# Spreading the short products of a Fourier stage between the long products of a matrix stage

## The chip, the cores and the metric

The kernel runs on one core of a Trainium2 chip. A core has five engines, each with a queue of its own: TensorE (PE in the profile; its weight loads are listed apart as PEld), VectorE (DVE), ScalarE (ACT), GpSimd (POOL) and SyncE (SP), which here only issues transfers. The metric is the device time of one execution in microseconds (us), from the first to the last instruction of the core. Every time below is either such a device time, or is read from a trace of one profiled execution. A product takes two operands: the one that stays in the array ("weights", loaded by a PEld instruction) and the one that streams through it, column by column.

## What is computed

Eight sequences of 3008 rows by 256 columns are transformed by a two-dimensional discrete Fourier transform, of which only the real part is kept. Each row of the result then goes through a two-layer network with a squared ReLU between.

```python
# x: (8, 3008, 256); w_in: (256, 2048); w_out: (2048, 256); all float32
X = np.fft.fft(np.fft.fft(x, axis=1), axis=2).real
t = X.reshape(8 * 3008, 256)
r = np.maximum(t @ w_in, 0.0)
out = (r * r) @ w_out
```

The kernel merges the transform along the 256 columns into `w_in` (the tables `G1` and `G2`). What is left of the transform, the one along the 3008 rows, is folded by sums and differences until only products of small cosine and sine tables are left; their results are joined again by sums and differences into two arrays, `Pt` and `Qt`. These are the streamed operand of the network.

## The kernel before

The main loop runs over 8 sequences, 6 blocks of 251 columns (the last has 250) and 8 pairs of hidden tiles `j`, 384 steps in all. A step has a `front` (four products of 251 columns, whose results VectorE combines), a `combine` on ScalarE and GpSimd, and a `back` (seven products of 251 columns), which belongs to the front of two steps earlier.

```python
def front(b, k0, n, j, between):
    ...
    for h in range(2):
        ...
        ps = psh.tile([P, 2, CH], F32, name="ph", tag="h")      # two buffers
        nc.tensor.matmul(hP, G1[:, fs], pt[:, ks], start=True, stop=True)
        nc.tensor.matmul(hQ, G2[0:P - 1, fs], qt[0:P - 1, ks], start=True, stop=True)
        nc.vector.scalar_tensor_tensor(out=t, in0=et[:, ks], scalar=gE[:, fc:fc + 1], in1=hP, ...)
        tt(out=g[:, h, 0, 0:n], in0=t, in1=hQ, op=ALU.add)
        tt(out=g[:, h, 1, 0:n][:, ::-1], in0=t, in1=hQ, op=ALU.subtract)
        between()
    return g
```

While sequence `b` goes through the network, sequence `b + 1` is transformed. Its work is a list `side` of pairs (weight, function), and `between()`, which each half of a front calls, takes from it. The weights set the pace: all of them together are spread evenly over a fixed number of calls (53 for the first list, 78 for each later one).

```python
def between():
    nonlocal spent
    if i < NJ + LAG or i % NJ == LAG - 1:
        return
    spent -= pace / 4 if i < 2 * NJ else pace
    while side and spent <= 0:
        t, f = side.pop(0)
        f()
        spent += t
...
    if i % per == 0:
        side = ahead(b + 1) if b + 1 < B else []
        calls = 2 * (NJ - 1) * (len(BLOCKS) - (0 if i else 2)) - 6 + (0 if i else (NJ - LAG) // 2)
        spent, pace = 0.0, sum(t for t, _ in side) / calls
```

The list begins with the folds, which are VectorE work for nearly all of it. For a tile of rows:

```python
        ops = [(0.9, f_s), (0.9, f_d), (0.7, f_sc), (0.6, f_dc), (1.1, f_w)]
        ...
        return ops + [(0.8, f_turn), (1.3 if odd else 0.7, f_even), (0.2, f_sine)], (1.4 if odd else 1.2, f_odd)
```

After them come four groups (`kp` 0 and 1, for the cosine and the sine). In each, `even_n` issues four products one after the other: one of row class 0 and one of class 1 (94 or 95 columns each), and two of class 2, each again of 94 or 95 columns, through `once_more`. `odd_n` issues four products of 188 or 189 columns. The `join` functions are VectorE sums and differences; `copy_4` is a ScalarE copy.

```python
            EVEN = ((0, 0, n2), (1, n2, n2), (2, 2 * n2, n1))

            def even_n():
                st["ps"] = psd.tile([P, 512], F32, name="pd", tag="d")[0:n]      # psd: two buffers
                for c, at, nk in EVEN:
                    if b and c == 2:
                        st["half"] = once_more(st["ps"][:, at:], c, nk)
                    else:
                        product(st["ps"][:, at:at + nk], c)
                copy_4()
            ...
            ops = [(0.1, even_n), (0.4, join_4), (0.5, join_2), (0.1, odd_n), (0.8, join_1)]
            if b and kp:
                ops.insert(4, (0.5, lambda: join_odd("odd", n0)))
                ops.insert(2, (0.4, lambda: join_odd("half", n1)))
            return ops
```

Sequence 0 has no side list; it is transformed before the loop starts. In the list for sequence 1 a small transform of one column of all later sequences (`b is None`, operand `we`, seven columns of weights) comes between the folds and the four groups.

Of the kernel before, what the change touches and what calls it, by code (L numbers as in the profile page):

```python
# [8 lines left out]
F32 = mybir.dt.float32  # L9
# [4 lines left out]
P = 128  # L14
# [68 lines left out]
def kernel(  # L83
# [43 lines left out]
    psd = ctx.enter_context(tc.tile_pool(name="psd", bufs=2, space=PSUM))  # L127
# [221 lines left out]
    def columns(tab, t, part):  # L349

        nk, at = NC[0][TILES[t][0]], PLACE[t]
        nq = (nk + 1) // 2
        return tab[:, 0, at + part * nq:at + (nk if part else nq)]
# [120 lines left out]
    def dft_ops(b):  # L474
# [7 lines left out]
        def group(kp, which):  # L482
            both_in = b == 0 and which == 1
            n = NE if b is None else P - 1 if which == 1 and b else P
            tab = sinT if which == 1 else cosT
            n2, _, n1, n0 = NC[kp]
            st = {}

            def product(ps, c, lone_e=False, only=None):

                ts = [t for t in range(NT) if TILES[t][0] == c]
                for t in ts if only is None else ts[only:only + 1]:
                    rows = TILES[t][3]
                    if b is None:
                        w = we[0:rows, kp, t, 0:n]
                    elif lone_e:
                        w = lone[0:rows, 2 * t + kp]
                    else:
                        w = folded[b, t][0:rows, kp, PART[which]]
                        w = w if which else w[:, 0:n]  # L500
                    nc.tensor.matmul(ps[0:w.shape[-1]], w,  # L501
                                     (cosT if lone_e else tab)[0:rows, kp, PLACE[t]:PLACE[t] + NC[kp][c]],
                                     start=t == ts[0] and (lone_e or not both_in), stop=t == ts[-1] and not lone_e,
                                     skip_group_check=both_in)

            EVEN = ((0, 0, n2), (1, n2, n2), (2, 2 * n2, n1))

            def even_n():
                st["ps"] = psd.tile([P, 512], F32, name="pd", tag="d")[0:n]
                for c, at, nk in EVEN:  # L510
                    if b and c == 2:
                        st["half"] = once_more(st["ps"][:, at:], c, nk)
                    else:
                        product(st["ps"][:, at:at + nk], c)
                copy_4()

            def copy_4():
                a = st["a"] = hp.tile([P, 2 * P], F32, name="da", tag="da", bufs=2)[0:n]
                nc.scalar.copy(a[:, 0:n2], st["ps"][0:n, 0:n2])
# [43 lines left out]
                    st["odd"] = pool.tile([P, 512], F32, name="pd", tag=tag)[:, 0:n0]  # L563
                product(st["odd"], 3, lone_e, i)

            def once_more(ps, c, nk):

                nq = (nk + 2) // 2 if kp else (nk + 1) // 2
                pairs, rows = ((((TWO, TWO + 1),), HALF2), (((ODD0, ODD0 + 1), (ODD0 + 2, NT)), P))[c == 3]
                for part in range(2):  # L570
                    if kp:
                        tab, o = (cosT, sinT)[part], 0
                        to = ps[:, part * nq:part * nq + nq]
                    else:
                        tab, o = (cosT, sinT)[which], part
                        to = ps[:, part:nk:2]
                    for i, pair in enumerate(pairs):
                        nc.tensor.matmul(to, folded[b, pair[part != which]][0:rows, kp, PART[which]][:, 0:n],  # L578
                                         columns(tab, pairs[0][i] if c == 3 else TWO, o)[0:rows],
                                         start=i == 0, stop=i == len(pairs) - 1)  # L580
                if not kp:
                    return ps[:, 0:nk]
                a = hp.tile([P, NC[0][3] // 2 + 1], F32, name="oc", tag="oc", bufs=1)[0:n, 0:nq]
                nc.scalar.copy(a, ps[:, 0:nq])
                return a, ps[:, nq:2 * nq]

            def odd_n():
                ps = psd.tile([P, 512], F32, name="pd", tag="d")[0:n]
                st["odd"] = ps[:, 0:n0]
                if b is None:  # L590
                    return product(ps[:, 0:n0], 3)
                st["odd"] = once_more(ps, 3, n0)

            def join_odd(what, nk):

                a, ps = st[what]
                nq = a.shape[-1]
                st[what] = o = hp.tile([P, NC[1][3]], F32, name="do", tag="do", bufs=1)[0:n, 0:nk]
                tt(out=o[:, 0::2], in0=a[:, 0:nq - 1], in1=ps[:, 0:nq - 1], op=ALU.add)
                if which == 1:  # L600
                    tt(out=o[:, 1::2], in0=ps[:, 1:nq], in1=a[:, 1:nq], op=ALU.subtract)
                else:
                    tt(out=o[:, 1::2], in0=a[:, 1:nq], in1=ps[:, 1:nq], op=ALU.subtract)
# [13 lines left out]
            if b == 0:  # L617
                named = [("join_4", join_4), ("join_2", join_2), ("lo", join_lo), ("hi", join_hi),
                         ("join_1", join_1)]
                for i in range(3):  # L620
                    for nm, f in (("even", even_part), ("odd", odd_part)):
                        named += [(nm + ("", "_e")[e] + str(i), lambda i=i, e=e, f=f: f(i, e == 1)) for e in range(2)]
                return [((which, kp, nm), f) for nm, f in named]
            ops = [(0.1, even_n), (0.4, join_4), (0.5, join_2), (0.1, odd_n), (0.8, join_1)]
            if b and kp:
                ops.insert(4, (0.5, lambda: join_odd("odd", n0)))
                ops.insert(2, (0.4, lambda: join_odd("half", n1)))
            return ops

        ops = [] if b is None else [(0.0, start)]  # L630
        for which in (2,) if b is None else (0, 1):
            for kp in range(2):
                ops += group(kp, which)
# [307 lines left out]
    for i in range(len(steps) + LAG + 4):  # L941
        if i < len(steps):
            b, k0, n, j = steps[i]
# [21 lines left out]
        if i >= LAG and flight:  # L965
            at, g_, s_ = flight.pop(0)
# [73 lines left out]
```

## Time and profile before

| what | value |
|---|---|
| device time, median of 3 runs | 1939.01 us (1938.49 to 1940.76) |
| span of the profiled run | 1936.6 us |
| VectorE busy | 1424.4 us, 74% |
| GpSimd busy | 1185.6 us, 61% |
| ScalarE busy | 939.5 us, 49% |

A line of instruction groups reads: source line, engine, operation, result <- operands, shape, count, then busy time in us and mean ns of one instruction. In a timeline the first two columns are start and length in us, and instructions of one kind that follow each other are merged into one line (`x4`). A float32 product is two matmul instructions in this trace, each with its own weight load; the text calls them passes. The end of a matmul is modelled by the profiler, so consecutive ones overlap in it; how long a pass really takes is read from the distance of starts. In a table by stretches (`A:B`) each engine has its busy time and, in brackets, its number of instructions.

### The profile page before, as it was taken

The page shows a single profiled execution, that of the slowest core. Times are in us where ns is not written, and L with a number is a line of the kernel's source. Part 1 is how long each engine was busy: PE and PEld are TensorE (multiplying, and loading weights), DVE is VectorE, ACT ScalarE, POOL GpSimd, SP SyncE. Part 2 cuts the span into 40 slices and gives each one's busy share as a digit, 9 for nine tenths or more (in the row PEclk, how much of TensorE's full clock was granted, in tenths as well). Part 3 has the DMA queues.
Part 4 walks back from the last instruction along what each step waited for, and adds up shares of the span by engine and source line. Part 5 has one row for each costly group of instructions (what it writes and reads, how often), then busy time and mean ns, then how long its engine had stood idle before and what let it go on. Part 6 is the DMA issues. An engine that isn't in the chain of part 4 may idle for free.

```text
span 1936.6 us, 27913 instructions
## 1 busy us (share of the span) xinstructions
PE 1922.7 (99%) x9266; PEld 1708.9 (88%) x9266; DVE 1424.4 (74%) x3502; ACT 939.5 (49%) x1134; POOL 1185.6 (61%) x1708
## 2 busy tenths in 40 slices
PE   8999999999999999999999999999999999999999
PEld 7788888888988899888998889888898888988887
DVE  8998867777677776787667776777767787655554
ACT  2855554544445544445444454445544454444443
POOL 0047646676567665766667665667756776556655
PEclk9999999999999999999999999999999999999999
DMA  8341101111011101111011100111001100000000
GB/s 216 115 48 41 39 8 51 33 32 27 27 41 31 38 12 30 39 41 28 11 35 47 36 20 11 42 48 28 20 17 52 33 11 22 28 12 11 22 11 22
DMA packets 145783, 69.56 MB, mean 36 GB/s; under 512 B 129309, under 2 KB 136423, under 8 KB 145638
## 3 DMA queue, kind: packets, MB, share of 16 engines
q1 hardware_dynamic: 145186, 66.87, 13.3%
q8 instruction: 73, 1.20, 0.3%
q0 software_dynamic: 176, 0.65, 0.1%
q14 instruction: 72, 0.59, 0.1%
q10 hardware_dynamic: 276, 0.26, 0.0%
HBM read 43.03 MB, written 24.69 MB: 35 GB/s over the span
## 4 chain that ended last, share of the span: by engine, by line
PE 95%; DVE 3%; DMA 1%; issue 0%; SPq 0%; ACT 0%; DVEq 0%
PE ph L664 17%; PE ph L665 16%; PE mC L717 16%; PE mA L717 16%; PE mB L717 16%; PE mD L717 8%; PE pd L578 2%; PE pd L501 1%; DMA cosT<-in_cos_s_dram 0%; DVE m L274 0%; DVE he L667 0%; DMA cosd<-in_cos_d_dram 0%; DVE fd L272 0%; DVE g L670 0%; PE mA L704 0%
## 5 line engine op out<-in xcount | busy, mean ns | idle before, releaser
L679 ACT ACTIVATE g<-g 128x1004 f32<-128x1004 f32 (+1 forms) x384 | 399.4, 1040 | 783.6 <-DVE g L670 419.1
L667 DVE SCALAR_TENSOR_TENSOR he<-Et,gE,ph 128x251 f32<-128x251 f32 (+1 forms) x768 | 361.6, 471 | 385.4 <-PE ph L665 382.0
L687 POOL TENSOR_TENSOR s<-g 128x251 f32<-128x251 f32 (+1 forms) x376 | 249.0, 662 | 640.6 <-ACT g L680 507.2
L664 PE MATMUL ph<-Pt,G 128*128 128x251 f32 (+1 forms) x1536 | 451.9, 375 | 0.2 <-DVE g L670 0.2
L665 PE MATMUL ph<-Qt,G 127*128 127x251 f32 (+1 forms) x1536 | 451.3, 374 | 0.0
L680 ACT ACTIVATE g<-g 128x1004 f32<-128x1004 f32 (+1 forms) x384 | 399.3, 1040 | 12.1
L717 PE MATMUL mC<-s,wsum 128*128 128x251 f32 (+1 forms) x1504 | 381.4, 374 | 0.0
L717 PE MATMUL mA<-g,wout 128*128 128x251 f32 (+1 forms) x1504 | 379.9, 374 | 0.0
L669 DVE TENSOR_TENSOR g<-he,ph 128x251 f32<-128x251 f32 (+1 forms) x768 | 320.5, 417 | 54.5 <-DVE he L667 0.9
L665 PEld LDWEIGHTS ph<-Qt,G 127*128 127x128 f32 x1536 | 291.3, 190 | 35.7
L664 PEld LDWEIGHTS ph<-Pt,G 128*128 128x128 f32 x1536 | 286.7, 189 | 36.2 <-DVE dc L547 1.3
L717 PEld LDWEIGHTS mC<-s,wsum 128*128 128x128 f32 x1504 | 285.5, 190 | 34.5
L670 DVE TENSOR_TENSOR g<-he,ph 128x251 f32<-128x251 f32 (+1 forms) x768 | 314.1, 409 | 0.0
L717 PEld LDWEIGHTS mA<-g,wout 128*128 128x128 f32 x1504 | 282.6, 189 | 35.0 <-issue 0.3
L689 POOL TENSOR_TENSOR s<-g 128x251 f32<-128x251 f32 (+1 forms) x376 | 303.3, 807 | 0.0
L688 POOL TENSOR_TENSOR s<-s,g 128x251 f32<-128x251 f32 (+1 forms) x376 | 280.1, 745 | 29.5
L690 POOL TENSOR_TENSOR s<-g,s 128x251 f32<-128x251 f32 (+1 forms) x376 | 260.6, 693 | 0.0
L717 PE MATMUL mB<-g,wsum 128*128 128x251 f32 (+1 forms) x752 | 220.4, 374 | 0.0
L717 PE MATMUL mD<-s,wout 128*128 128x251 f32 (+1 forms) x752 | 220.3, 374 | 0.0
L717 PE MATMUL mB<-s,wout 128*128 128x251 f32 (+1 forms) x752 | 219.9, 374 | 0.0
L717 PEld LDWEIGHTS mB<-g,wsum 128*128 128x128 f32 x752 | 142.5, 190 | 17.5
L717 PEld LDWEIGHTS mD<-s,wout 128*128 128x128 f32 x752 | 141.9, 189 | 17.7
(139 smaller groups left out, 1353.9 us busy)
## 6 DMA issues: line engine op xcount, KB each, us to landing
out_dram<-os SPq DMA_DIRECT2D x376, 56.0 KB
xt<-in_x_dram SPq DMA_DIRECT2D x25, 384.0 KB
xt<-in_x_dram SPq DMA_DIRECT2D x63, 128.0 KB
Et<-e_dram SPq DMA_DIRECT2D x7, 752.5 KB
xt<-in_x_dram SPq DMA_DIRECT2D x9, 512.0 KB
out_dram<-os SPq DMA_DIRECT2D x288, 6.8 KB
raw<-in_moe_w_in_dram SPq DMA_DIRECT2D x16, 256.0 KB
raw<-in_moe_w_out_dram SPq DMA_DIRECT2D x16, 256.0 KB
```

Source lines behind the costliest of these rows:

```text
L664: nc.tensor.matmul(hP, G1[:, fs], pt[:, ks], start=True, stop=True)
L665: nc.tensor.matmul(hQ, G2[0:P - 1, fs], qt[0:P - 1, ks], start=True, stop=True)
L667: nc.vector.scalar_tensor_tensor(out=t, in0=et[:, ks], scalar=gE[:, fc:fc + 1], in1=hP, op0=ALU.mult, op1=ALU.add)
L669: tt(out=g[:, h, 0, 0:n], in0=t, in1=hQ, op=ALU.add)
L670: tt(out=g[:, h, 1, 0:n][:, ::-1], in0=t, in1=hQ, op=ALU.subtract)
L679: act(v, v, AF.Relu)
L680: act(v, v, AF.Square)
L687: gt(out=s1, in0=g21, in1=g22, op=ALU.add)
L688: gt(out=s2, in0=s1, in1=g11, op=ALU.subtract)
L689: gt(out=s3, in0=g11, in1=g21, op=ALU.subtract)
L690: gt(out=s4, in0=g12, in1=s2, op=ALU.subtract)
L717: nc.tensor.matmul(acc[nm][:, i, 0:n], w, v[:, 0:n], start=j == 0 and i == 0, stop=j == NJ - 1, skip_group_check=True)
```

## The change

The lists of sequences 1 to 7 no longer have `even_n`. In its place stand four entries, each with one product of 94 or 95 columns and a weight of 0.6, so that `between()` hands them out at different calls, with products of 251 columns between them, as far as the pace allows. `even_n` stays for the small transform of one column. The products, their operands and their order are unchanged; `copy_4` comes after the second product and not after the fourth. The aim is that the weight loads of the short products and of what follows them can lie beside longer products. Since 2.4 stands in each group where 0.1 stood, the sum of the weights grows too, and with it the pace at which the whole list is handed out.

```diff
             def even_n():
                 st["ps"] = psd.tile([P, 512], F32, name="pd", tag="d")[0:n]
                 for c, at, nk in EVEN:
-                    if b and c == 2:
-                        st["half"] = once_more(st["ps"][:, at:], c, nk)
-                    else:
-                        product(st["ps"][:, at:at + nk], c)
+                    product(st["ps"][:, at:at + nk], c)
                 copy_4()
+            def even_0():
+                st["ps"] = psd.tile([P, 512], F32, name="pd", tag="d")[0:n]
+                product(st["ps"][:, 0:n2], 0)
+
+            def even_1():
+                product(st["ps"][:, n2:2 * n2], 1)
+                copy_4()
+
+            def half(part):
+                c, at, nk = EVEN[2]
+                st["half"] = once_more(st["ps"][:, at:], c, nk, part)
 ...
-            def once_more(ps, c, nk):
+            def once_more(ps, c, nk, only=None):
 ...
-                for part in range(2):
+                for part in range(2) if only is None else (only,):
 ...
-                if not kp:
+                if not kp or only == 0:
                     return ps[:, 0:nk]
 ...
-            ops = [(0.1, even_n), (0.4, join_4), (0.5, join_2), (0.1, odd_n), (0.8, join_1)]
-            if b and kp:
-                ops.insert(4, (0.5, lambda: join_odd("odd", n0)))
-                ops.insert(2, (0.4, lambda: join_odd("half", n1)))
-            return ops
+            ops = [(0.4, join_4), (0.5, join_2), (0.1, odd_n), (0.8, join_1)]
+            if not b:
+                return [(0.1, even_n)] + ops
+            if kp:
+                ops.insert(3, (0.5, lambda: join_odd("odd", n0)))
+                ops.insert(1, (0.4, lambda: join_odd("half", n1)))
+            return [(0.6, even_0), (0.6, even_1), (0.6, lambda: half(0)), (0.6, lambda: half(1))] + ops
```

## The prediction

> **What bounds the kernel now.** I read the page's first lines, then the waits of the steady part, then the timeline of TensorE around one group of short products, and last the table by stretches for VectorE.
>
> ```profile
> PE 1922.7 (99%) x9266; PEld 1708.9 (88%) x9266; DVE 1424.4 (74%) x3502; ACT 939.5 (49%) x1134; POOL 1185.6 (61%) x1708
> PE 95%; DVE 3%; DMA 1%; issue 0%; SPq 0%; ACT 0%; DVEq 0%
> ```
>
> The second line is the chain of work that ended last: 95% of the span is TensorE waiting for itself. The waits of the stretch from 480 to 1900 us say the same from the other side. All twenty lines of that answer have ScalarE, VectorE or GpSimd as the one that waits; the longest ones are these, and no PE or PEld line is among them:
>
> ```profile
> POOL s L687 <- ACT g L680: 400.3, 229, 4.4
> ACT g L679 <- DVE g L670: 335.2, 142, 4.2
> DVE he L667 <- PE ph L665: 321.5, 246, 3.0
> ```
>
> So in sequences 2 to 7 TensorE never waits for another engine. There the time is the sum of what its passes take, and a change can help only by making passes shorter. How long they take stands in the timeline (PE, then PEld) around one `even_n`:
>
> ```profile
> 466.05 0.58 PE L664 MATMUL ph<-Pt,G 128*128 128x251 f32 x2
> 466.47 0.59 PE L665 MATMUL ph<-Qt,G 127*128 127x251 f32 x2
> 466.90 0.58 PE L501 MATMUL pd<-cosT,w 95*128 95x95 f32 x4
> 467.32 0.61 PE L578 MATMUL pd<-cosT,w 94*128 94x95 f32 x4
> 467.76 0.62 PE L664 MATMUL ph<-Pt,G 128*128 128x251 f32 x2
> 468.22 0.59 PE L665 MATMUL ph<-Qt,G 127*128 127x251 f32 x2
> 468.64 0.59 PE L717 MATMUL mA<-g,wout 128*128 128x251 f32 x2
> ```
>
> ```profile
> 466.26 0.40 PEld L665 LDWEIGHTS ph<-Qt,G 127*128 127x128 f32 x2
> 466.69 0.62 PEld L501 LDWEIGHTS pd<-cosT,w 95*128 95x128 f32 x4
> 467.23 0.53 PEld L578 LDWEIGHTS pd<-cosT,w 94*128 94x128 f32 x4
> 467.68 0.30 PEld L664 LDWEIGHTS ph<-Pt,G 128*128 128x128 f32 x2
> ```
>
> A product of 251 columns takes 466.47 - 466.05 = 0.42 us for two passes; over longer stretches a pass is 0.212 us, which is 0.847 ns a column. A product of 189 columns (`odd_n`, at 477.14 us: eight passes in 1.28 us) takes 0.160 us a pass, again 0.847 ns a column. A pass of 95 columns would then take 0.080 us. It takes more: within the row the starts are 0.111 us apart (by end times, the eight distances here are 83, 111, 113, 111, 112, 112, 110, 112 ns, and the long pass after the row comes 243 ns after the last short one in place of 212). Eight passes and the two long ones after them need 468.22 - 466.90 = 1.32 us; taking off 0.425 leaves 0.895 us for the eight. So the row costs 0.895 - 8 x 0.080 = 0.25 us more than its columns. This is what the change is after.
>
> The reader is to see where in the row this excess arises. The first short pass is at full speed (83 ns): its weights were loaded during the long pass before it. Each weight load starts when the pass before it starts, 466.69 beside the long pass at 466.68 and so on, and never earlier. The excess therefore lies behind each short pass, not in front of it: a pass of 0.080 us is too short a cover for the next load, which needs 0.111. Eight short passes, eight such excesses of 31 ns; the eighth is paid by the long product behind the row (243 for 212).
>
> **What the Trainium skill says.** The page TensorE: Matmul & The Clock Gate, section Step-by-step: what each phase is for, says that a weight load can be pulled ahead of running matmuls into a background buffer, so that the next weights load while the present product runs. The trace agrees, and shows one load ahead, no more. The same page, section LDWEIGHTS (loading the stationary operand), gives columns / 1.2 ns whatever the number of rows: 107 ns for 128 columns. The trace has 111 ns as the distance in a row of short passes, with 94 and with 95 rows alike, though it lists each load with about 190 ns. The page Perfetto Trace Analysis, section Identifying the Most-Contended Engine, warns that matmul busy time isn't a measure of the distance to the best possible, and I use distances of starts for that reason.
>
> **The change part by part.**
>
> 1. Short products alone. One product is two short passes. Put between long ones, the first runs at 83.5 ns, the second ends 111.3 ns later (it loads its weights behind the first), and the long pass after it ends 242 ns later (its weights load behind the second). Together 436.8, less 212.4 for the long pass: 224.4 ns a product, 898 for four. The row of four today: 83.5 + 7 x 111.3 + 242 - 212.4 = 892 ns. So nothing is hidden that wasn't hidden: the number of passes that follow a short pass is eight in both. If anything, each new row adds 2 ns at its entry. With the weights and calls given I worked the lists through: for sequences 2 to 7 twelve of the sixteen short products come alone and four in pairs, 14 rows in place of 4; for sequence 1 most come in pairs. About 66 more rows at 2 ns: +0.1 us.
>
> 2. The pace in sequences 2 to 7. The weights add to 49.1 before and 58.3 after (4 x 2.3 more); over 78 calls the pace goes from 0.63 to 0.75, so the folds are handed out 19% more densely, and end earlier. VectorE has room: these rows of the table by stretches are the folds of sequence 3 and the groups after them,
>
> ```profile
> core 0: us, PE busy (x) PEld busy (x) DVE busy (x) ACT busy (x) POOL busy (x), PEclk, DMA share, GB/s
> 515.00:700.00 185.00, 185.00 (x874) 164.70 (x873) 140.51 (x333) 90.24 (x100) 126.46 (x177) 1.00 0.13 36
> 700.00:748.00 48.00, 48.00 (x250) 43.69 (x250) 32.59 (x91) 22.05 (x32) 26.24 (x40) 1.00 0.05 12
> ```
>
> 76% busy in the folds. The front's three operations (0.47, 0.42 and 0.41 us, about 1.3 a call, 2.34 us of TensorE apart) are some 100 of the 140 us; the other 40 grow by a fifth to 48 in the same time, 80%. No wait, 0 us.
>
> 3. The pace in sequence 1's list. Its weights are 56.2 before and 65.4 after, over only 53 calls: 1.06 and 1.23. Here VectorE is close to its limit already:
>
> ```profile
> 142.00:182.00 40.00, 40.00 (x190) 35.58 (x189) 35.22 (x83) 21.01 (x26) 28.34 (x38) 1.00 0.25 63
> 182.00:232.00 50.00, 49.81 (x237) 43.78 (x236) 44.49 (x106) 27.84 (x37) 36.92 (x52) 1.00 0.10 27
> ```
>
> 79.7 of 90 us, and the one wait of TensorE for VectorE of the whole loop (0.46 us at 188.8 us, where `f_sc` and `f_odd` come at one call). Fronts, gathers and stores are some 56 of the 79.7; the remaining 23 grow by 16%, +3.8 us, to 93%. I followed VectorE's queue call by call with the durations of the trace (front 1.19 us a half, each fold operation at its own), with TensorE free to go on until the second `ph` buffer is missing. It gives 0.4 us of waits before, as seen, and 1.85 after. With 1.16 or 1.22 for the front it gives 1.0 and 1.85 us more. I take +1.4 us.
>
> 4. The small transform. At each entry and exit of products with 7 columns of weights TensorE loses about 0.1 and 0.2 us (by end times the passes at 231.6 and 232.7 us come 98 and 196 ns late). With the new pace two of the four visits fall into one call: -0.3 us.
>
> 5. `psd` has two buffers, so `even_0` waits until `join_2` of the group before has read its tile. Before, one of 28 rows waits so, 0.13 us at 278.6. In sequence 1 the joins are closer now: +0.2 us. In the others there is a call or more between.
>
> Sum: 0.1 + 0 + 1.4 - 0.3 + 0.2 = +1.4 us; 1939.0 + 1.4 = 1940.4.
>
> **The rivals.** First, the loads are hidden after all, as the change intends: if a long product before or behind let TensorE load two sets of weights ahead, the excess would go, 28 rows x 8 x 31 ns = -6.9 us in all, and 1932 to 1934 with the waits of sequence 1. For it speaks only that a load may run ahead in principle. Against it: of the loads that I looked at none starts before the pass ahead of it, even behind long passes with 0.1 us of spare time.
>
> Second, VectorE becomes the bound in sequence 1: if the denser folds also slow GpSimd's and VectorE's operations (the same `w` operation has 505 ns in one form and 883 in another), the waits might come to 4 or 5 us: 1943 to 1944. Against it: the folds end earlier by the same amount, and a late `g` has two steps until `back` needs it.
>
> Third, the joins wait more: a tile is held over four calls more. That costs no TensorE time unless the next group catches up with it, which the lists show in sequence 1 alone.
>
> **Range and chances.** The sum gives 1940.4; the runs before spread over 2.3 us themselves. I put 1 in 10 on a hidden load (below 1937) and less than 1 in 10 on waits of over 3 us. Range 1937 to 1943. 2% would be 39 us, six times the whole excess: faster 0.01, same 0.985, slower 0.005.
>
> **What would show it.** Right: in the timeline of a product that is alone, ends at about 83 and 111 ns and the long pass after it at 242; 224 passes of 94 and 95 columns after 250 us as before, and a period of sequences 2 to 7 that is the same within 0.1 us (before, the same row of short products starts at 466.90 and at 699.84 us: 232.94 us). New waits of PE for VectorE `g` (`ph` L664) between 142 and 232 us, 1 to 3 us in all. Wrong: a long pass after a short one that ends 212 ns behind it, a period shorter by 0.5 us or more, or waits of TensorE on a join in the later sequences.

## The result and the profile after

The changed kernel takes 1953.70 us (median of 6 runs, 1953.34 to 1954.14) against 1939.18 us before: a ratio of 1.0073, 95% interval 1.006 to 1.0086. That is 14.5 us or 0.7% slower, and far above the range of the prediction (1937 to 1943).

The page of the changed kernel, its busy times and its chain of work:

```profile
PE 1930.3 (99%) x9266; PEld 1712.9 (88%) x9266; DVE 1421.1 (73%) x3502; ACT 941.0 (48%) x1134; POOL 1176.6 (60%) x1708
PE 91%; DVE 6%; ACT 1%; DMA 1%; issue 1%; SPq 0%; DVEq 0%; ACTq 0%
```

TensorE looks as full as before, 99%. The chain tells more: TensorE's share fell from 95% to 91%, VectorE's rose from 3% to 6% and ScalarE's from 0% to 1%. It only points, since 4% of the span would be 78 us and 14.5 are lost. The waits of TensorE's weight loads from 100 to 1900 us name the places (who waited for what, us in total, times, longest; the first four lines):

```profile
PEld pd L588 <- ACT da L529: 7.1, 8, 2.6
PEld ph L676 <- DVE g L682: 3.6, 5, 1.2
PEld pd L501 <- issue: 3.3, 14, 0.3
PEld pd L501 <- DVE we L372: 3.1, 1, 3.1
```

The first line did not exist before: products of `half` (L588) wait for `copy_4` (L529). The fourth is the small transform, which waits for the fold of its column. First, a short product that is alone, and the new wait beside it (TensorE, the list of sequence 2):

```profile
496.32 0.58 PE L676 MATMUL ph<-Pt,G 128*128 128x251 f32 x2
496.74 0.59 PE L677 MATMUL ph<-Qt,G 127*128 127x251 f32 x2
497.17 0.36 PE L501 MATMUL pd<-sinT,w 94*127 94x95 f32 x2
497.36 0.62 PE L676 MATMUL ph<-Pt,G 128*128 128x251 f32 x2
497.81 0.59 PE L677 MATMUL ph<-Qt,G 127*128 127x251 f32 x2
498.77 0.68 PE L588 MATMUL pd<-sinT,w 94*127 94x95 f32 x4 [0.37 <-ACT da L529]
```

From 497.17 to 497.81 us lie one short product and one long one: 0.64 us, less 0.42 for the long one leaves 0.22 us. A quarter of the old row was 0.895 / 4 = 0.224. By end times it is 84, 111 and 242 ns in the mean of the 72 lone products of sequences 2 to 7, as in the row. The next short products should start 0.42 us after 497.81, at 498.23; they start at 498.77. ScalarE in the same stretch:

```profile
496.48 1.04 ACT L691 ACTIVATE g<-g 128x1004 f32<-128x1004 f32 x1 [4.74 <-DVE g L682]
497.55 1.04 ACT L692 ACTIVATE g<-g 128x1004 f32<-128x1004 f32 x1
498.50 0.22 ACT L529 COPY da<-pd 127x95 f32<-127x95 f32 x1
```

The copy could have run at 497.5, when its product was done. It stands in ScalarE's queue behind a ReLU and a square, and TensorE waits for the end of it. The longest wait for the copy is in sequence 1 (lines left out):

```profile
247.46 0.36 PE L501 MATMUL pd<-cosT,w 94*128 94x95 f32 x2
...
250.02 0.23 ACT L529 COPY da<-pd 128x95 f32<-128x95 f32 x1
...
250.31 0.46 PE L588 MATMUL pd<-cosT,w 94*128 94x95 f32 x2 [2.49 <-ACT da L529]
```

The copy stands there behind six ScalarE operations that prepare tables, from 247.56 us on.

Second, sequence 1, the end of its folds (all engines, lines left out):

```profile
213.93 0.59 PE L677 MATMUL ph<-Qt,G 127*128 127x251 f32 x2
...
215.29 0.69 PE L676 MATMUL ph<-Pt,G 128*128 128x251 f32 x2 [0.77 <-DVE g L682]
...
215.82 0.59 PE L677 MATMUL ph<-Qt,G 127*128 127x251 f32 x2
...
217.37 0.35 ACT L368 ACTIVATE xe<-xe 128x196 f32<-128x196 f32 x1
...
217.75 0.59 DVE L370 TENSOR_TENSOR es<-xe 128x98 f32<-128x98 f32 x1 [1.28 <-ACT xe L368]
...
218.37 1.38 DVE L372 TENSOR_TENSOR we<-es 128x49 f32<-128x49 f32 x2
...
219.13 2.06 PE L501 MATMUL pd<-cosT,we 95*7 95x95 f32 x8 [2.73 <-DVE we L372]
```

Between 215.82 and 219.13 TensorE has only two passes to do. It waits for a chain of four pieces: ReLU and square on ScalarE, then the doubling of the column (L368), then VectorE's folds of it (L370, L372). And what comes after the wait is slow. The same visit of eight passes took 1.14 us in the kernel before; this one takes 2.06. Before:

```profile
231.12 0.59 PE L665 MATMUL ph<-Qt,G 127*128 127x251 f32 x2
231.63 1.14 PE L501 MATMUL pd<-cosT,we 95*7 95x95 f32 x8
```

The table by stretches of the changed kernel shows why (third figure from the right is the granted clock):

```profile
core 0: us, PE busy (x) PEld busy (x) DVE busy (x) ACT busy (x) POOL busy (x), PEclk, DMA share, GB/s
142.00:182.00 40.00, 40.00 (x188) 35.12 (x187) 37.78 (x88) 21.14 (x25) 26.98 (x37) 1.00 0.23 63
215.00:220.00 5.00, 1.98 (x9) 1.32 (x10) 3.58 (x8) 2.33 (x3) 2.47 (x5) 0.83 0.00 0
220.00:226.00 6.00, 6.00 (x18) 4.31 (x17) 1.67 (x5) 2.21 (x3) 2.65 (x5) 0.57 0.00 0
226.00:232.00 6.00, 6.00 (x30) 5.34 (x29) 3.62 (x10) 2.79 (x4) 1.26 (x3) 1.00 0.00 0
```

In smaller stretches the clock is 0.50 from 218.3 to 225.1 us, and a long pass took 0.419 us in place of 0.212. TensorE's busy share is 100% from 220 to 226 us: this loss isn't seen in it at all.

The whole sum, from the distance of the same products in both traces (the spans differ by 14.9 us):

| where | cause | us |
|---|---|---|
| sequences 2 to 7 | wait for `copy_4`, once in each, 0.51 to 0.63 | +3.2 |
| sequence 1 | wait for `copy_4`, at 250.3 (2.76) and 289.8 (0.60) | +3.35 |
| sequence 1 | wait for the folded column | +2.9 |
| sequence 1 | lowered clock after that wait | +2.8 |
| sequence 1 | waits for `g`, 2.94 in place of 0.46 | +2.5 |
| sequence 1 | wait for a join, 0.59 in place of 0.14 | +0.45 |
| sequence 1 | one visit of narrow products fewer | -0.3 |
| all | excess behind short passes, 0.97 to 0.99 a sequence in both | 0 |

### The profile page after: what moved, and what is told of

Same layout as the page of the kernel before. It is cut to its first block, busy times and chain, and to the rows that moved or that the text cites. A ratio compares the mean times of both kernels' runs of the same rounds, so it can differ in the third digit from the quotient of the medians.

```text
span 1951.5 us, 27926 instructions
## 1 busy us (share of the span) xinstructions
PE 1930.3 (99%) x9266; PEld 1712.9 (88%) x9266; DVE 1421.1 (73%) x3502; ACT 941.0 (48%) x1134; POOL 1176.6 (60%) x1708
## 4 chain that ended last, share of the span: by engine, by line
PE 91%; DVE 6%; ACT 1%; DMA 1%; issue 1%; SPq 0%; DVEq 0%; ACTq 0%
PE mA L729 16%; PE mC L729 16%; PE mB L729 16%; PE ph L676 16%; PE ph L677 16%; PE mD L729 8%; PE pd L588 2%; PE pd L501 1%; DVE he L679 1%; DVE g L682 1%; DVE g L681 1%; DMA cosT<-in_cos_s_dram 0%; ACT g L691 0%; DVE m L274 0%; ACT g L692 0%
## 5 line engine op out<-in xcount | busy, mean ns | idle before, releaser
L699 POOL TENSOR_TENSOR s<-g 128x251 f32<-128x251 f32 (+1 forms) x376 | 249.6, 664 | 661.0 <-ACT g L692 514.8
L681 DVE TENSOR_TENSOR g<-he,ph 128x251 f32<-128x251 f32 (+1 forms) x768 | 320.5, 417 | 53.6 <-DVE he L679 1.4
L701 POOL TENSOR_TENSOR s<-g 128x251 f32<-128x251 f32 (+1 forms) x376 | 295.6, 786 | 0.0
L702 POOL TENSOR_TENSOR s<-g,s 128x251 f32<-128x251 f32 (+1 forms) x376 | 254.6, 677 | 0.0
```

What stands on the lines that cost most here:

```text
L699: gt(out=s1, in0=g21, in1=g22, op=ALU.add)
L701: gt(out=s3, in0=g11, in1=g21, op=ALU.subtract)
L702: gt(out=s4, in0=g12, in1=s2, op=ALU.subtract)
```

## The experiments

The theory that I put to the test: new waits make the whole loss (and the clock that falls after one of them), and spread short products cost and save nothing. Its rivals are that a lone product costs more than one in a row, that it saves time which the waits cover, and that the pace has no part in it. All ratios are to the kernel before, run beside.

**Where the copy stands.** The changed kernel with `copy_4` after the fourth product.

```diff
             def even_1():
                 product(st["ps"][:, n2:2 * n2], 1)
-                copy_4()
             def half(part):
                 c, at, nk = EVEN[2]
                 st["half"] = once_more(st["ps"][:, at:], c, nk, part)
+                if part == 1:
+                    copy_4()
```

> The changed kernel, but the ScalarE copy of the group's tile comes after the fourth short product again and not after the second. Theory W (three new waits make the loss; the lone products themselves cost nothing): the products of class 2 go to the tile that the copy reads, so they wait for it; with the copy last that wait is gone. Sequences 2 to 7 fall from 233.5 to 232.95 us each (-3.2 in all), sequence 1 loses 2.76 + 0.59 us of waits: about 1947 us, with no wait of TensorE for the copy. Rival L (a lone product costs more than one in a row): 1953 to 1954, the periods stay at 233.5.

Measured: 1945.96 us (ratio 1.0038, 1.0024 to 1.0051): 7.2 us over the kernel before, in place of 14.5. The period of a later sequence is 232.94 or 232.99 us, against 232.93 or 232.98 before, and the same list of waits has no line with `da` any more; the waits in sequence 1 for `g` and for the column stayed:

```profile
PEld ph L677 <- DVE g L683: 4.0, 6, 1.1
PEld pd L501 <- issue: 3.5, 13, 0.6
PEld pd L501 <- DVE we L372: 3.1, 1, 3.1
```

So the copy's new place cost about 7 us. The copy reads columns 0 to 94 of the tile and `half` writes from column 188 on. They don't touch, but the program makes the later write wait for the earlier read of the same tile. As long as the copy came after all four products there was nothing to wait for.

**Sequence 1 as before, the others changed.**

```diff
-            return [(0.6, even_0), (0.6, even_1), (0.6, lambda: half(0)), (0.6, lambda: half(1))] + ops
+            four = (even_0, even_1, lambda: half(0), lambda: half(1))
+            if b == 1:
+                return [(0.1, lambda: [f() for f in four])] + ops
+            return [(0.6, f) for f in four] + ops
...
```

In sequence 1 `copy_4` also comes after the fourth product again.

> Sequence 1 has its four products in a row and its old weights again; sequences 2 to 7 stay as in the changed kernel. Theory W: all of sequence 1's loss (11.7 us) goes, 0.52 to 0.64 us remain in each of the six others: about 1942.4 us. Rival L: the loss is in proportion to the groups, of which 24 of 28 remain changed: about 1951.

Measured: 1942.16 us (1.0017, 1.0011 to 1.0024). 24 of 28 groups are still changed and 3.4 us of 14.5 are left. The loss is not in proportion to the spread products.

**Both together.** As the last one, with the copy after the fourth product everywhere.

> Both at once: in sequences 2 to 7 the short products are spread and the pace is denser, but the copy comes last; sequence 1 is as before. What is left of the change is lone short products and the denser pace where VectorE has room. Theory W: 1939.2 us, within 0.5 of the kernel before, periods of 232.95 us. Rival H (lone products do hide their loads and the waits covered it): 24 groups x 0.25 us less, 1933. Rival L: 1942 or more.

Measured: 1938.91 us against 1938.74 (1.0000, 0.9991 to 1.0008). In six of seven sequences the short products are spread and the list is handed out 19% faster, and the time is that of the kernel before within 0.1%; the periods are 232.94 and 232.99 us by turns, against 232.93 and 232.98 (one of them is 233.11, with a small wait for `g`). This answers the question that the change asked: 24 groups x 0.25 us = 6.0 us would have shown (0.3%), and nothing did.

**The pace alone.** The kernel before with one number changed.

```diff
-            ops = [(0.1, even_n), (0.4, join_4), (0.5, join_2), (0.1, odd_n), (0.8, join_1)]
+            ops = [(2.4 if b else 0.1, even_n), (0.4, join_4), (0.5, join_2), (0.1, odd_n), (0.8, join_1)]
```

> The kernel before with one number changed: the row of four products has the weight 2.4 in place of 0.1, so the list is handed out at the pace of the changed kernel and nothing is spread. Theory W: sequence 1 has the waits for VectorE (about +1.8 us), the wait of the small transform for its folded column (3 us) and the TensorE clock lowered after it (about 3.5 us), less 0.6 us at entries and exits; the later sequences nothing: about 1947 us. Rival S (the spreading alone makes the loss, the pace is harmless): 1939 to 1940.

Measured: 1947.66 us (1.0047, 1.0033 to 1.0061). No product is moved away from its neighbours here, and 8.9 us are lost. In its trace nearly all of that arises while sequence 1 is transformed. The later sequences, where nothing was expected, lose about 0.1 us each in a small wait for `g`. Its timeline of TensorE has the same waits at the same place as the changed kernel, 3.3 us from the second line to the third and again a visit of 2 us:

```profile
215.06 0.69 PE L664 MATMUL ph<-Pt,G 128*128 128x251 f32 x2 [0.77 <-DVE g L670]
215.59 0.59 PE L665 MATMUL ph<-Qt,G 127*128 127x251 f32 x2
218.91 2.06 PE L501 MATMUL pd<-cosT,we 95*7 95x95 f32 x8 [2.73 <-DVE we L372]
```

**The column folded earlier.** The changed kernel, with the 1.5 of `fold_columns` moved ahead of the last tile's folds.

```diff
-            groups = [(1.5, fold_columns)] + dft_ops(None) + tables + groups
+            groups = dft_ops(None) + tables + groups
...
+            if b == 1 and ops[0] is start:
+                pieces.insert(-9, (1.5, fold_columns))
```

> The changed kernel, with the fold of the one column (1.5 of weight, same sum) moved from just ahead of the small transform to before the last tile's folds. Theory W: TensorE no longer waits 2.98 us for it at 219 us, and if the lowered clock from 219 to 224 us follows from that wait it goes too (about 3 us): 1947 to 1948 us, clock 1.00 in that stretch. Rival C (the clock falls for another reason, such as the 1 us waits before): 1950 to 1951, and the clock is still below 0.9 there.

Measured: 1948.11 us (1.0048, 1.0034 to 1.0062). The small transform starts without a wait, its first visit takes 1.14 us as in the kernel before, and the clock is full:

```profile
214.56 0.59 PE L677 MATMUL ph<-Qt,G 127*128 127x251 f32 x2
215.08 1.14 PE L501 MATMUL pd<-cosT,we 95*7 95x95 f32 x8
216.15 1.11 PE L729 MATMUL mA<-g,wout 128*128 128x251 f32 x4
```

```profile
215.00:220.00 5.00, 5.00 (x27) 4.06 (x27) 4.05 (x12) 4.07 (x8) 3.59 (x4) 1.00 0.00 0
220.00:226.00 6.00, 6.00 (x29) 4.88 (x28) 4.45 (x12) 3.48 (x5) 4.54 (x7) 1.00 0.00 0
```

The lowered clock went with the wait. At 9.4 us over the kernel before in place of 14.5, the early fold saved 5.1 us.

**Both mends.** The changed kernel with the early fold and the late copy, in all seven sequences.

> The changed kernel with both mends, the early fold of the column and the copy after the fourth product; all of the change is otherwise in it, in all seven sequences. Theory W: what remains over the kernel before is the waits for VectorE in sequence 1 (2.5 to 4 us, the moved fold adds to the VectorE work in its place) and one wait for a join (0.6 us), less 0.6 us of entries and exits: 1941 to 1942.5 us. If lone products hid their loads, it would be 1935 or less.

Measured: 1940.35 us (1.0011, 1.0002 to 1.0019), just under the range expected. In the trace 1.9 us over the kernel before arise in sequence 1: waits for `g` of 1.98 us against 0.46, and the join's 0.59 against 0.14, with small terms beside them. (That trace is of the slowest of twelve executions, 1942.86 us; it was 2.55 us behind already at step 16.)

**A try for something better.** Two entries and exits of narrow products fewer, in the kernel before.

```diff
         if b is None:
+            (_, e0), a0, c0, (_, o0), d0, (_, e1), a1, c1, (_, o1), d1 = ops
+            ops = [(0.2, lambda: (e0(), e1())), a0, c0, a1, c1, (0.2, lambda: (o0(), o1())), d0, d1]
             ops.append((0.0, lambda: nc.sync.dma_start(out=e_dram[1:, :], in_=PQE[1][2][0:NE])))
```

> The kernel before, with the small transform's products of 7 weight columns issued in two visits and not in four. Each entry and exit of such products costs TensorE 0.10 + 0.20 us in the kernel before: -0.6 us in the trace of sequence 1, 1938.2 us. Rival: the wait for a join that the second visit then has (its tile is freed by a join) takes it back, 1938.7.

Measured: 1940.08 us against 1938.67 (1.0006, 0.9998 to 1.0015): no gain, and above both figures expected, though the interval does not tell it from the kernel before. The trace does: two entries and exits are saved, a wait for the join takes back more, and 1.4 us are lost in sequence 1:

```profile
239.02 0.59 PE L667 MATMUL ph<-Qt,G 127*128 127x251 f32 x2
241.21 4.05 PE L501 MATMUL pd<-cosT,we 128*7 128x377 f32 x12 [1.60 <-DVE dc L547]
```

No version that beats the kernel before came out of these runs.

## Why the prediction was wrong

The sum was 1940.4 us, and 1953.70 was measured. Two steps failed: step 4 left out what the small transform waits for (5.7 us with the clock that it lowers), and step 5 the wait for the copy (6.5 us).

**Short products alone (step 1): right.** 0.224 us a product was predicted and measured, 84, 111 and 242 ns by ends, and the run "Both together" shows a ratio of 1.0000. The mechanism, one load ahead and one excess behind each short pass wherever it stands, held: from 60 us on no load of the traces before and after starts earlier than the pass ahead of it.

**The pace in sequences 2 to 7 (step 2): right for VectorE.** TensorE never waits for `g` there in the changed kernel. With the same pace and the products in a row it does, 0.1 us a sequence, so "no wait" was right by a small margin.

**The pace in sequence 1 (step 3): right in kind, too small in size.** The term was +1.4 us and measured +2.5. VectorE's share rose as predicted, to 37.78 of 40 us (94%) before 182 us. The wait of 1.03 us at 214 us follows a call with `f_turn` and `f_even`, which held VectorE for 2.49 us (the front before leaves it at 211.51, the next starts at 214.00). In the kernel before the same three operations come at two calls, with a front between them (0.87 us from 223.65, 1.68 us from 225.69). How the prediction's working placed and timed them is not on record, so why the term came out too small stays open.

**The small transform (step 4): this term failed.** I counted the visits (-0.3 us, as measured) and not what the visit waits for. In both kernels `fold_columns` and the first narrow product stand at neighbouring calls, but there are two kinds of neighbours. Before, they were the second call of one step and the first of the next, with nine long products (3.8 us) between. After, they are both calls of one step, with two long products (0.85 us) between. The chain from ReLU (215.35 us) to folded column takes 3.8 us. Wait 2.9 and clock 2.8, +5.7 us; the pace-only run shows that this comes from the pace.

**The tile (step 5): this step failed.** I asked who frees the buffer that `even_0` takes (the join: +0.2 predicted, +0.45 measured) and did not ask what the diff's smallest move does, the copy from behind the fourth product to behind the second. It made a reader between two writers of one tile. In sequences 2 to 7 it cost once and not four times: only one of the four groups has `even_1` and `half(0)` at the two calls of one step. In sequence 1 the two waits are in the groups that have them at one and the same call. 3.35 + 3.2 = 6.5 us, confirmed by the run with the late copy (7.3 us less, with the noise of both).

**The rivals.** The hidden loads are refuted. VectorE as the bound in sequence 1 had the right stage, but was put at 4 or 5 us of waits and came to 2.94, between it and the 1.85 of the main working; whether denser folds slow VectorE's operations stays open. The third, joins, cost 0.45 us. The rival that came true, ScalarE's queue on TensorE's path, was not in the list. The range was too narrow because it covered the known terms and nothing for waits that I had not listed.

## What to carry to other kernels

Here, where each weight load starts with the pass ahead of it, spreading short products between long ones saved nothing (ratio 1.0000): each short pass of 80 ns leaves 31 ns of the next load uncovered, whichever product that load belongs to. When a block of work is cut into pieces, list for every piece what it now waits for, also a reader that has come between two writers of a tile, and how much of the bounding engine's work lies between producer and consumer at the new places. A pacing weight is a change of its own: test it alone before judging what it was meant to serve.

## What was not expected of the hardware

After two waits of TensorE, of 1.03 us (to 215.29 us) and of 2.9 us (to 219.13 us), the granted clock was 0.50 from 218.3 to 225.1 us, and this lost as much again as the second wait. Length alone doesn't settle when it happens: after the wait of 2.76 us at 250 us of the same run there was none. And after a wait of 2.3 us that ends at 53.6 us, in the part that all kernels share, the clock fell in the changed kernel (0.50 from 54.5 to 57.9 us) but stayed at 1.00 in the kernel before.

The traces say more. In all nine of them each lowered stretch that starts after 20 us and ends before the kernel is 3.41 or 6.83 us long, and within a trace they start a whole number of times 3.413 us apart (54.48 and 218.32 us here: 163.84 us, 48 times). With the trace cut into pieces of 3.41 us on this grid (in the kernel before it is taken from the one change of its clock, at 1936.44 us), the piece ahead of a lowered stretch stands out:

| kernel | piece, us | TensorE busy, us | clock in the next piece |
|---|---|---|---|
| changed | 51.07 to 54.48 | 1.15 | 0.50 |
| changed | 214.91 to 218.32 | 1.11 | 0.50 |
| changed | 245.63 to 249.04 | 2.19 | 1.00 |
| changed | 249.04 to 252.45 | 2.15 | 1.00 |
| before | 48.87 to 52.29 | 2.49 | 1.00 |
| before | 52.29 to 55.70 | 2.08 | 1.00 |

After 20 us the nine traces have some 5000 pieces at full clock. In 19 of them, nine at the ends of the kernels, TensorE is busy for 1.60 us or less, and each is followed by a lowered clock; none of the others, with 1.81 us or more, is. So the same wait lowers the clock or not by where the grid cuts it, which differs from execution to execution: the edge at 249.04 us halves the wait of 2.76 us, and the edge at 52.29 us the early one of the kernel before. This is read from the traces; no run was made to test it.

In the changed kernel the early fall cost nothing that lasted (0.05 us at step 16), since VectorE bounds that stage (busy for 40.06 of the 42 us from 58 to 100 us).
